# A batch-normalised convolution on one core: a shorter start-up, parameters in PSUM, and one weight sum moved to VectorE by way of PSUM

## The chip, the cores and the metric

The kernel runs on one core of a Trainium2 chip. The metric is the device time of one execution in microseconds (us). The kernel before was timed three times: 195.16, 195.81 and 196.03 us, a median of 195.81 us. The core has five engines that each take their instructions strictly in the order in which the kernel issues them: TensorE (PE in the profile; its weight loads are listed as PEld), VectorE (DVE), ScalarE (ACT), GpSimd (POOL) and SyncE (SP), which here only issues DMAs. A semaphore holds an instruction back until the instructions that it depends on are done, and with it everything behind it on its engine.

## The reference

A convolution of width 3 along the sequence, then a batch norm with stored statistics, then SiLU. All inputs are bf16.

```
B, S, C = 2, 2048, 1024
K = 3
xp = jnp.pad(x, ((0, 0), (P, P), (0, 0)))                      # P = K // 2 = 1
y = sum(jnp.einsum('bsc,cd->bsd', xp[:, k:k + S, :], w[k]) for k in range(K))
inv_std = 1.0 / jnp.sqrt(var + 1e-5)
y = (y - mean) * (g * inv_std) + b
return _silu(y)
```

## The kernel before

The convolution is computed in a transformed domain. Six outputs along the sequence are one tile; a batch of 2048 rows has NTB = 342 tiles. Each tile's 8 input rows are turned into 8 values (points j = 0 to 7) by the 8 x 8 matrix BT, the three weight taps are turned into 8 weight matrices, the products over the 1024 input channels are taken point by point, and 8 products give back 6 outputs. That is 8 products of [1024 x 1024] for 6 rows in place of 18.

**Set-up.** `Rm` (lines 99 to 136) is BT laid out as a [128, 8, 21] matrix, so that one matmul transforms a window of 127 or 128 rows of x, that is 21 tiles, for 128 channels. POOL writes index differences (`val`, line 101), VectorE turns them into an indicator `E` (line 104) and builds rows 1 to 6 of `Rm` from it in 25 small multiply-adds (line 116); POOL writes rows 0 and 7 (line 128) and the identity `ident`. `xw0`, the first window, needs a zero first row, which POOL clears (line 98).

**First stage: the transform of batch 0** (lines 337 to 353). For each of 17 windows, SP loads 128 rows of x (lines 202, 203, 206), TensorE does 8 matmuls (line 216, one for each block of 128 channels, four of them in two PSUM banks), and ScalarE (line 230) or VectorE (line 232) copies the halves to `T_sb` as bf16. The weights of the first output chunk (128 output channels; three taps, `load_chunk`, line 88) are loaded after windows 1 and 2, and the four parameter vectors by POOL's queue (line 178). `turn_params` (line 180), issued ahead of the last window, transposes the parameters in PSUM on TensorE, and VectorE copies them to SBUF (`prmT`, line 183); `make_params` (line 185) computes scale and bias on POOL.

**Weights.** For each chunk dc, `pair_weights` (line 153) makes six transformed weight matrices `uch` of [128, 8 x 128] in three pairs, on POOL: e1 = w0 + w2, then e1 + w1 and e1 - w1; e2 = w0 + 4 w2, then e2 + 2 w1 and e2 - 2 w1; eh = 4 w0 + w2, then eh + 2 w1 and eh - 2 w1. The multiples (`w2x`, `w1x`, `w0x`) are made by `scale_weights` (line 141) on ScalarE, for chunk 0 on POOL. Points 0 and 7 use w0 and w2 as they are.

**Second stage and the rest.** A `unit` (line 251) is one chunk and one batch: 64 matmuls (line 241) of 342 columns, eight for each point, in the order 1, 3, 2, 4, 5, 7, 6, 0, into columns 0 to 341 of four PSUM banks (A, B_, C_, G); units take the lower and the upper four banks in turn. ScalarE copies some products out (line 280) and VectorE combines them with multiply-adds (line 273) into six output rows `y`; the last two of these in a unit write `y[0]`. ScalarE applies scale, bias and SiLU (line 317), partly after the next unit has begun (`late`), the DMA queue transposes, and SP stores. The first unit, (0, 0), is interleaved with the transform of batch 1 (lines 361 to 371), 52 of its matmuls spread over the 17 windows. Then come the units (0, 1), (1, 0), (1, 1) to (7, 1), all bound in order on TensorE (lines 415 to 432). Ahead of each unit (dc, 1), `open_chunk`, `pair_weights` and `scale_weights` issue the weight work of chunk dc + 1 (lines 418 to 427); it stands in each engine's queue behind the work of unit (dc, 0) and ahead of that of unit (dc, 1). The order of all instructions is the order of the program's text (`manual_schedule`, line 60); the framework adds the semaphore waits. `ps_all` (line 69) is a single tile over all 8 banks of PSUM.

Of the kernel before, what the change touches and what calls it, by code (L numbers as in the profile page):

```python
# [9 lines left out]
ALU = mybir.AluOpType  # L10
FP32 = mybir.dt.float32
BF16 = mybir.dt.bfloat16
# [4 lines left out]
BT = [  # L17
# [8 lines left out]
]  # L26
C1 = -2.0 / 9.0
# [3 lines left out]
NJ = 8  # L31
WT = 21
# [3 lines left out]
def kernel(  # L36
# [50 lines left out]
    def load_chunk(dc, k):  # L87
        nc.sync.dma_start(out=raw[dc][k], in_=w_all[:, k, :, dc * P:(dc + 1) * P])  # L88

    open_weights(0)  # L90

    dummy = consts.tile([P, 2], FP32, name="dummy")
    nc.vector.memset(dummy, 0.0)
    nc.scalar.activation(dummy[:, 1:2], dummy[:, 0:1], ACT.Silu)


    xw0 = consts.tile([P, C], BF16, name="xw0")
    nc.gpsimd.memset(xw0[0:1, :], 0.0)
    Rm = consts.tile([P, NJ, WT], BF16, name="Rm")
    val = consts.tile([P, NJ, WT], I32, name="val")  # L100
    nc.gpsimd.iota(val, pattern=[[-1, NJ], [-M_OUT, WT]], base=0, channel_multiplier=1)
    E = consts.tile([P, NJ, WT], FP32, name="E")
    nc.vector.memset(Rm, 0.0)
    nc.vector.tensor_single_scalar(E, val, 0.0, op=ALU.is_equal)
    for k in range(NJ):
        j = 1
        while j < 7:
            v = BT[j][k]
            if v == 0:
                j += 1  # L110
                continue
            j1 = j
            while j1 + 1 < 7 and BT[j1 + 1][k] == v:
                j1 += 1
            nj = j1 - j + 1
            nc.vector.scalar_tensor_tensor(  # L116
                out=Rm[:, j:j1 + 1, :],
                in0=E[:, k:k + 1, :].to_broadcast([P, nj, WT]) if nj > 1 else E[:, k:k + 1, :],
                scalar=float(v),
                in1=Rm[:, j:j1 + 1, :],  # L120
                op0=ALU.mult,
                op1=ALU.add,
            )
            j = j1 + 1
# [12 lines left out]
    ident = consts.tile([P, P], BF16, name="ident")  # L137
    make_identity(nc, ident)
    yTs = [consts.tile([P, M_OUT, NP], BF16, name=f"yT{i}") for i in range(2)]

    def scale_weights(dc, taps=(2, 1, 0), on_gpsimd=False):
        for k in taps:
            f = 2.0 if k == 1 else 4.0
            dst = wx[dc, k] = wtmp.tile([P, CT, P], BF16, name=f"w{k}x")
            if on_gpsimd:
                nc.gpsimd.tensor_scalar(dst, raw[dc][k], f, 0.0, op0=ALU.mult, op1=ALU.add)
            else:
                nc.scalar.mul(dst, raw[dc][k], f)  # L148

    def open_chunk(dc):  # L150
        wts[dc] = upool.tile([P, 6, CT, P], BF16, name="uch")

    def pair_weights(dc, n):

        w0, w1, w2 = raw[dc]
        e = wtmp.tile([P, CT, P], FP32, name=("e1", "e2", "eh")[n])
        a = wx[dc, 0] if n == 2 else w0
        c = wx[dc, 2] if n == 1 else w2
        odd = wx[dc, 1] if n else w1
        nc.gpsimd.tensor_tensor(e, a, c, op=ALU.add)  # L160
# [4 lines left out]
    load = {"act": 0.0, "dve": 1.0}  # L165
    EVAC = {"act": (0.17, 0.14), "dve": (0.12, 0.17)}

    prm = consts.tile([4 * DC, P], BF16, name="prm")
    prmT = consts.tile([P, 4, DC], FP32, name="prmT")
# [6 lines left out]
    def load_params():  # L176
        for q, ap in enumerate((var, g, mean, b)):
            nc.gpsimd.dma_start(out=prm[q * DC:(q + 1) * DC, :], in_=ap.rearrange("(dc p) -> dc p", p=P))

    def turn_params(bk):  # L180
        pv = ps_all[:, bk * 512:bk * 512 + 2 * DC].bitcast(BF16)
        nc.tensor.transpose(pv, prm, ident[0:4 * DC, 0:4 * DC])
        nc.vector.tensor_copy(prmT.rearrange("p q d -> p (q d)"), pv)

    def make_params():
        nc.gpsimd.memset(mhalf, -0.5)
        nc.gpsimd.tensor_scalar(rstd, prmT[:, 0, :], 1e-5, 1.0, op0=ALU.add, op1=ALU.mult)
        nc.gpsimd.tensor_tensor(rstd, rstd, mhalf, op=ALU.pow)
        nc.gpsimd.tensor_tensor(sc, prmT[:, 1, :], rstd, op=ALU.mult)
        nc.gpsimd.tensor_tensor(beta, prmT[:, 2, :], sc, op=ALU.mult)  # L190
        nc.gpsimd.tensor_tensor(beta, prmT[:, 3, :], beta, op=ALU.subtract)
        nc.gpsimd.tensor_scalar(sk, sc, C1, 0.0, op0=ALU.mult, op1=ALU.add)

    epool = ctx.enter_context(tc.tile_pool(name="epool", bufs=1))

    def load_window(xpool, bi, wi):
        ntile = min(WT, NTB - WT * wi)
# [138 lines left out]
    with tc.tile_pool(name="xwin", bufs=10) as xpool:  # L336
        for wi in range(NWIN):
            window = load_window(xpool, 0, wi)
            if wi == 1:
                load_chunk(0, 0)  # L340
                load_chunk(0, 2)
                load_params()
            if wi == 2:
                load_chunk(0, 1)
            for h in range(2):
                transform(0, wi, window, 4 * h, 4, (2 * wi + h) % 4 * 2, 2)
            if wi == 5:
                open_chunk(0)
                for n, taps in ((0, ()), (1, (2, 1)), (2, (0,))):
                    scale_weights(0, taps, on_gpsimd=True)  # L350
                    pair_weights(0, n)
            if wi == NWIN - 2:
                turn_params((2 * wi + 2) % 4 * 2)
        make_params()
        for yT in yTs:
            nc.gpsimd.memset(yT[:, :, NTB:NP], 0.0)

        first = unit(0, 0, 0, NTB, (0, 1, 2, 3), yTs[0], late, seven_first=True)
        load["act"] = load["dve"] = 0.0
        gi, done = 0, 0  # L360
        for wi in range(NWIN):
            window = load_window(xpool, 1, wi)
            if wi == 6:
                for k in (0, 2, 1):
                    load_chunk(1, k)
            for ct0, n in ((0, 3), (3, 3), (6, 2)):
                transform(1, wi, window, ct0, n, 4 + gi % 4, 3)
                gi += 1
                want = 52 * gi // (3 * NWIN)
                run(first, want - done)  # L370
                done = want
        load_weights(1)
        run(first)
# [146 lines left out]
```

## Time and profile before

| What | Value |
|---|---|
| timed runs | 195.16, 195.81, 196.03 us |
| the profiled execution's own time | 196.92 us |
| its span, first to last instruction | 195.1 us |
| granted TensorE clock, mean | 0.979 |
| TensorE busy | 177.8 us (91%) |
| POOL busy | 164.7 us (84%) |
| VectorE busy | 149.4 us (77%) |
| ScalarE busy | 124.2 us (64%) |
| HBM read and written | 14.82 and 8.39 MB |

The span is 1.8 us shorter than the execution's own time, and that execution was 1.1 us longer than the median of the timed runs. A busy share is a mean over stages with different limits: TensorE waits in the first 23 us and in the last 10, and hardly between. In the views that follow, a row gives the start and the length in us, the engine, the line of the code, the operation with its output and inputs, how many instructions are merged in it, and in brackets the idle time ahead of it with what ended it.

### The profile page before, as it was taken

What the parts mean: (1) busy time and instruction counts of PE and PEld (TensorE: products, weight loads), DVE (VectorE), ACT (ScalarE), POOL (GpSimd) and SP (SyncE); (2) the same over time, 40 slices, a digit from 0 to 9 for tenths busy, and PEclk for the clock granted to TensorE, in tenths of its full rate; (3) what the DMA queues carried; (4) which work ended last, traced back from release to release, by engine and by line L of the source; (5) the groups of instructions that cost most, each with busy time, mean ns of one, the idle gap of its engine ahead of it and who ended that gap; (6) DMA issues with size and microseconds to landing.
All of it is one profiled execution on the core that took longest, in us unless ns stands there. A gap on an engine that the chain in (4) does not pass through costs nothing.

```text
span 195.1 us, 3898 instructions
## 1 busy us (share of the span) xinstructions
PE 177.8 (91%) x1397; PEld 126.7 (65%) x1397; DVE 149.4 (77%) x345; ACT 124.2 (64%) x206; POOL 164.7 (84%) x105
## 2 busy tenths in 40 slices
PE   0779799989999999999999999999999999999840
PEld 0668588856666666666666666666666666679830
DVE  6369668996878696969696969686877878697880
ACT  3479558878378827873786287548736872827930
POOL 7899999999999999999999999999999999800000
PEclk9999879999999999999999999999999999999995
DMA  4999999900607487999292989774755657397505
GB/s 135 277 392 344 332 257 371 284 15 2 116 5 137 96 159 182 276 166 200 39 211 41 198 229 257 142 157 92 139 112 116 129 105 152 76 174 157 115 5 108
DMA packets 86823, 31.72 MB, mean 163 GB/s; under 512 B 73428, under 2 KB 82644, under 8 KB 86804
## 3 DMA queue, kind: packets, MB, share of 16 engines
q1 hardware_dynamic: 86637, 31.46, 69.8%
q8 instruction: 11, 0.18, 0.3%
q14 instruction: 8, 0.07, 0.1%
q0 software_dynamic: 128, 0.01, 0.0%
q10 hardware_dynamic: 39, 0.01, 0.0%
HBM read 14.82 MB, written 8.39 MB: 119 GB/s over the span
## 4 chain that ended last, share of the span: by engine, by line
PE 84%; DVE 7%; DMA 3%; SPq 2%; ACT 1%; issue 1%; DVEq 0%; ACTq 0%
PE ps_all L241 76%; PE ps_all L216 7%; DVE T_sb L232 4%; DMA xw<-in_x_dram 3%; DVE y L273 1%; SPq L206 1%; SPq L88 1%; PE ps_all L446 1%; DVE o_end L478 1%; DVE o_end L486 0%; ACT m L280 0%; ACT yT L317 0%; SPq L203 0%; SPq L202 0%; DVE ps_all L273 0%
## 5 line engine op out<-in xcount | busy, mean ns | idle before, releaser
L241 PE MATMUL ps_all<-T_sb,uch 128*128 128x342 bf16 (+2 forms) x816 | 123.9, 299 | 1.8 <-ACT m L280 1.8
L241 PEld LDWEIGHTS <-uch 128*128 128x128 bf16 x816 | 76.7, 97 | 34.5 <-issue 1.3
L317 ACT ACTIVATE yT<-y,beta,sk 128x684 bf16<-128x684 f32 (+8 forms) x51 | 47.1, 925 | 29.9 <-DVE y L273 29.8
L273 DVE SCALAR_TENSOR_TENSOR y<-ps_all,y 128x342 f32<-128x342 f32 (+2 forms) x102 | 45.4, 487 | 1.3
L241 PE MATMUL ps_all<-T_sb,wch 128*128 128x342 bf16 (+2 forms) x272 | 44.7, 303 | 0.1
L216 PE MATMUL ps_all<-Rm,xw 128*128 128x168 bf16 (+1 forms) x272 | 31.8, 248 | 8.5 <-DVE Rm L116 5.4
L280 ACT COPY m<-ps_all 128x342 f32<-128x342 f32 (+2 forms) x51 | 21.7, 427 | 20.6 <-PE ps_all L241 19.6
L230 ACT CAST T_sb<-ps_all 128x672 bf16<-128x672 f32 (+5 forms) x45 | 26.2, 606 | 13.0 <-PE ps_all L216 12.0
L216 PEld LDWEIGHTS <-xw 128*128 128x128 bf16 (+1 forms) x272 | 24.1, 104 | 14.9 <-POOL ident masks.py:199 5.4
L241 PEld LDWEIGHTS <-wch 128*128 128x128 bf16 x272 | 26.0, 98 | 11.6 <-DVE T_sb L232 0.3
L232 DVE CAST T_sb<-ps_all 128x672 bf16<-128x672 f32 (+3 forms) x40 | 26.1, 698 | 8.4 <-PE ps_all L216 8.2
L273 DVE SCALAR_TENSOR_TENSOR d<-m,ps_all 128x342 f32<-128x342 f32 (+2 forms) x17 | 8.3, 490 | 21.0 <-ACT s L280 21.0
L273 DVE SCALAR_TENSOR_TENSOR y<-ps_all,d 128x342 f32<-128x342 f32 (+2 forms) x51 | 22.0, 486 | 0.6
L273 DVE SCALAR_TENSOR_TENSOR y<-ps_all,s 128x342 f32<-128x342 f32 (+2 forms) x34 | 15.2, 489 | 6.3 <-ACT s L280 6.3
L161 POOL TENSOR_TENSOR uch<-e,w1x 128x1024 bf16<-128x1024 f32 x8 | 17.0, 2131 | 1.2 <-ACT w1x L148 0.7
L160 POOL TENSOR_TENSOR e<-wch 128x1024 f32<-128x1024 bf16 x8 | 17.0, 2125 | 0.8 <-DMA wch<-in_w_dram 0.8
L161 POOL TENSOR_TENSOR uch<-eh,w1x 128x1024 bf16<-128x1024 f32 x8 | 17.0, 2131 | 0.6
L161 POOL TENSOR_TENSOR uch<-e,wch 128x1024 bf16<-128x1024 f32 x8 | 17.0, 2129 | 0.6
L160 POOL TENSOR_TENSOR e<-wch,w2x 128x1024 f32<-128x1024 bf16 x8 | 17.0, 2125 | 0.3 <-ACT w2x L148 0.2
L160 POOL TENSOR_TENSOR eh<-w0x,wch 128x1024 f32<-128x1024 bf16 x8 | 17.0, 2124 | 0.1
L162 POOL TENSOR_TENSOR uch<-e,wch 128x1024 bf16<-128x1024 f32 x8 | 17.1, 2133 | 0.0
L162 POOL TENSOR_TENSOR uch<-eh,w1x 128x1024 bf16<-128x1024 f32 x8 | 17.1, 2132 | 0.0
(46 smaller groups left out, 113.6 us busy)
## 6 DMA issues: line engine op xcount, KB each, us to landing
xw<-in_x_dram SPq DMA_DIRECT2D x30, 256.0 KB
out_dram<-o_sb SPq DMA_DIRECT2D x28, 192.0 KB
wch<-in_w_dram SPq DMA_DIRECT2D x9, 512.0 KB
out_dram<-o_sb SPq DMA_DIRECT2D x14, 120.0 KB
wch<-in_w_dram SPq DMA_DIRECT2D x6, 256.0 KB
xw<-in_x_dram SPq DMA_DIRECT2D x2, 224.0 KB
out_dram<-o_before SPq DMA_DIRECT2D x2, 192.0 KB
o_sb<-yT SPq DMA_TRANSPOSE x14
```

The source lines that it names most:

```text
L88: nc.sync.dma_start(out=raw[dc][k], in_=w_all[:, k, :, dc * P:(dc + 1) * P])
L160: nc.gpsimd.tensor_tensor(e, a, c, op=ALU.add)
L161: nc.gpsimd.tensor_tensor(wts[dc][:, 2 * n], e, odd, op=ALU.add)
L162: nc.gpsimd.tensor_tensor(wts[dc][:, 2 * n + 1], e, odd, op=ALU.subtract)
L206: nc.sync.dma_start(out=xw[0:kk, :], in_=x[bi, t_lo:t_hi + 1, :])
L216: nc.tensor.matmul(banks[:, at:at + NJ * ntile], lhsT=xw[0:kk, (ct0 + c) * P:(ct0 + c + 1) * P], rhs=Rm[0:kk, :, 0:ntile], start=True, sto ...
L230: nc.scalar.copy(dst, src)
L232: nc.vector.tensor_copy(dst, src)
L241: nc.tensor.matmul(ps_all[:, bk * 512:bk * 512 + c1 - c0], lhsT=lhsT, rhs=T_sb[bi][:, ct, j, c0:c1], start=start and ct == 0, stop=ct == C ...
L273: nc.vector.scalar_tensor_tensor(out=o, in0=i0, scalar=s, in1=i1, op0=ALU.mult, op1=op1)
L280: nc.scalar.copy(dst, src)
L317: nc.scalar.activation(yT[:, i0:i1:2, c0:c1], y_all[:, i0:i1:2], ACT.Silu, bias=beta[:, dc:dc + 1], scale=sk[:, dc:dc + 1],)
```

## The change: what it does

- **A shorter build of `Rm`.** Rows 1 to 6 come in pairs with equal even and opposite odd parts. Each pair now takes four multiply-adds by way of a helper tile `parts`, 12 in all for the 25. Only rows 0 and 7 are cleared first. The zero row of `xw0` is cleared by VectorE after the build, not by POOL ahead of it.
- **Parameters.** Their four loads go to ScalarE's queue at the very start, ahead of its table load. The transpose follows window 0. The transposed parameters stay in PSUM, in columns 496 to 511 of bank 0, and are read there. VectorE adds the epsilon, POOL takes the power, and VectorE computes scale and bias after the last window.
- **Dummy matmuls.** A zeroed tile `warm` and seven matmuls of 512 columns into bank 7, ahead of the first window.
- **First weights.** The three loads of chunk 0 are issued after windows 3, 5 and 7 instead of 1, 1 and 2; their pair work is issued after window 7 instead of 5.
- **The second pair's sum** for chunks 1 to 7: ScalarE writes 4 w2 as fp32 to columns 352 to 479 of all eight PSUM banks, and VectorE adds w0 to it. POOL's addition for this pair is gone, and so is the `w2x` multiple. ScalarE's multiples of w1 and w0 are now issued ahead of all three pairs.
- **Smaller things.** The clearing of the padding in `yTs` moves to the start of POOL's queue, and the first unit's matmuls are spread one transform group later.

```diff
+    prm = consts.tile([4 * DC, P], BF16, name="prm")
+    for q, ap in enumerate((var, g, mean, b)):
+        nc.scalar.dma_start(out=prm[q * DC:(q + 1) * DC, :], in_=ap.rearrange("(dc p) -> dc p", p=P))
+
     dummy = consts.tile([P, 2], FP32, name="dummy")
...
-    xw0 = consts.tile([P, C], BF16, name="xw0")
-    nc.gpsimd.memset(xw0[0:1, :], 0.0)
     Rm = consts.tile([P, NJ, WT], BF16, name="Rm")
     val = consts.tile([P, NJ, WT], I32, name="val")
     nc.gpsimd.iota(val, pattern=[[-1, NJ], [-M_OUT, WT]], base=0, channel_multiplier=1)
+    xw0 = consts.tile([P, C], BF16, name="xw0")
     E = consts.tile([P, NJ, WT], FP32, name="E")
-    nc.vector.memset(Rm, 0.0)
+    parts = consts.tile([P, 3, 2, WT], FP32, name="parts")
+    warm = consts.tile([P, 512], BF16, name="warm")
+    nc.vector.memset(warm, 0.0)
+    nc.vector.memset(Rm[:, 0:NJ:NJ - 1, :], 0.0)
     nc.vector.tensor_single_scalar(E, val, 0.0, op=ALU.is_equal)
-    for k in range(NJ):
...
+    for n, odd in enumerate((1.0, 2.0, 0.5)):
+        row = BT[2 * n + 1]
+        assert [odd * row[k + 1] for k in (1, 3, 5)] == row[1:6:2] and row[6] == 1
+        rstt(parts[:, n], E[:, 1:3], row[2], E[:, 5:7])
+        rstt(parts[:, n], E[:, 3:5], row[4], parts[:, n])
+        rstt(Rm[:, 2 * n + 1], parts[:, n, 0], odd, parts[:, n, 1])
+        rstt(Rm[:, 2 * n + 2], parts[:, n, 0], -odd, parts[:, n, 1])
+    nc.vector.memset(xw0[0:1, :], 0.0)
...
+    for yT in yTs:
+        nc.gpsimd.memset(yT[:, :, NTB:NP], 0.0)
...
-        c = wx[dc, 2] if n == 1 else w2
+        c = wx[dc, 2] if n == 1 and not dc else w2
         odd = wx[dc, 1] if n else w1
-        nc.gpsimd.tensor_tensor(e, a, c, op=ALU.add)
+        if n == 1 and dc:
+            four = ps_all.rearrange("p (k e) -> p k e", e=512)[:, :, 352:352 + P]
+            nc.scalar.mul(four, w2, 4.0)
+            nc.vector.scalar_tensor_tensor(out=e, in0=four, scalar=1.0, in1=w0, op0=ALU.mult, op1=ALU.add)
+        else:
+            nc.gpsimd.tensor_tensor(e, a, c, op=ALU.add)
         nc.gpsimd.tensor_tensor(wts[dc][:, 2 * n], e, odd, op=ALU.add)
         nc.gpsimd.tensor_tensor(wts[dc][:, 2 * n + 1], e, odd, op=ALU.subtract)
...
-    def turn_params(bk):
-        pv = ps_all[:, bk * 512:bk * 512 + 2 * DC].bitcast(BF16)
-        nc.tensor.transpose(pv, prm, ident[0:4 * DC, 0:4 * DC])
-        nc.vector.tensor_copy(prmT.rearrange("p q d -> p (q d)"), pv)
+    prmT = ps_all[:, 512 - 2 * DC:512].bitcast(BF16).rearrange("p (q d) -> p q d", q=4)
+
+    def turn_params():
+        nc.tensor.transpose(prmT.rearrange("p q d -> p (q d)"), prm, ident[0:4 * DC, 0:4 * DC])
+        nc.vector.tensor_scalar(rstd, prmT[:, 0, :], 1e-5, 1.0, op0=ALU.add, op1=ALU.mult)
+        nc.gpsimd.tensor_tensor(rstd, rstd, mhalf, op=ALU.pow)
 
     def make_params():
...
+        nc.vector.tensor_tensor(sc, prmT[:, 1, :], rstd, op=ALU.mult)
+        nc.vector.tensor_tensor(beta, prmT[:, 2, :], sc, op=ALU.mult)
+        nc.vector.tensor_tensor(beta, prmT[:, 3, :], beta, op=ALU.subtract)
+        nc.vector.scalar_tensor_tensor(out=sk, in0=prmT[:, 1, :], scalar=C1, in1=rstd, op0=ALU.mult, op1=ALU.mult)
+
+    nc.gpsimd.memset(mhalf, -0.5)
...
+    for _ in range(7):
+        nc.tensor.matmul(ps_all[:, 7 * 512:8 * 512], lhsT=warm[:, 0:P], rhs=warm, start=True, stop=True)
...
-            if wi == 1:
-                load_chunk(0, 0)
-                load_chunk(0, 2)
-                load_params()
-            if wi == 2:
-                load_chunk(0, 1)
+            if wi in (3, 5, 7):
+                load_chunk(0, {3: 0, 5: 2, 7: 1}[wi])
             for h in range(2):
                 transform(0, wi, window, 4 * h, 4, (2 * wi + h) % 4 * 2, 2)
-            if wi == 5:
+            if wi == 0:
+                turn_params()
+            if wi == 7:
...
-            if wi == NWIN - 2:
-                turn_params((2 * wi + 2) % 4 * 2)
         make_params()
...
-                want = 52 * gi // (3 * NWIN)
+                want = 52 * max(gi - 1, 0) // (3 * NWIN - 1)
...
             open_chunk(dc + 1)
-            pair_weights(dc + 1, 0)
-            if dc == 0:
-                scale_weights(1, (2,), on_gpsimd=True)
-                scale_weights(1, (1, 0))
-            else:
-                scale_weights(dc + 1)
-            for n in (1, 2):
+            scale_weights(dc + 1, (1, 0))
+            for n in range(3):
                 pair_weights(dc + 1, n)
```

More of the change, by code (lines that the diff above doesn't have):

```diff
@@ L101, with rstt @@
     nc.gpsimd.iota(val, pattern=[[-1, NJ], [-M_OUT, WT]], base=0, channel_multiplier=1)
+    xw0 = consts.tile([P, C], BF16, name="xw0")
     E = consts.tile([P, NJ, WT], FP32, name="E")
-    nc.vector.memset(Rm, 0.0)
+    parts = consts.tile([P, 3, 2, WT], FP32, name="parts")
+    warm = consts.tile([P, 512], BF16, name="warm")
+    nc.vector.memset(warm, 0.0)
+    nc.vector.memset(Rm[:, 0:NJ:NJ - 1, :], 0.0)
     nc.vector.tensor_single_scalar(E, val, 0.0, op=ALU.is_equal)
-    for k in range(NJ):
[L106 to L124, printed above, removed]
+    def rstt(o, i0, f, i1):
+        nc.vector.scalar_tensor_tensor(out=o, in0=i0, scalar=float(f), in1=i1, op0=ALU.mult, op1=ALU.add)
+    for n, odd in enumerate((1.0, 2.0, 0.5)):
[6 more added lines that the diff above has]
+    nc.vector.memset(xw0[0:1, :], 0.0)
     for j in (0, 7):
@@ L166 @@
     EVAC = {"act": (0.17, 0.14), "dve": (0.12, 0.17)}
-    prm = consts.tile([4 * DC, P], BF16, name="prm")
-    prmT = consts.tile([P, 4, DC], FP32, name="prmT")
     sk = consts.tile([P, DC], FP32, name="sk")
@@ L174 @@
     sc = consts.tile([P, DC], FP32, name="sc")
-    def load_params():
-        for q, ap in enumerate((var, g, mean, b)):
-            nc.gpsimd.dma_start(out=prm[q * DC:(q + 1) * DC, :], in_=ap.rearrange("(dc p) -> dc p", p=P))
-    def turn_params(bk):
-        pv = ps_all[:, bk * 512:bk * 512 + 2 * DC].bitcast(BF16)
-        nc.tensor.transpose(pv, prm, ident[0:4 * DC, 0:4 * DC])
-        nc.vector.tensor_copy(prmT.rearrange("p q d -> p (q d)"), pv)
-    def make_params():
[L186 to L192, printed above, removed]
+    prmT = ps_all[:, 512 - 2 * DC:512].bitcast(BF16).rearrange("p (q d) -> p q d", q=4)
[3 more added lines that the diff above has]
+        nc.gpsimd.tensor_tensor(rstd, rstd, mhalf, op=ALU.pow)
+    def make_params():
+        nc.vector.tensor_tensor(sc, prmT[:, 1, :], rstd, op=ALU.mult)
[3 more added lines that the diff above has]
+    nc.gpsimd.memset(mhalf, -0.5)
     epool = ctx.enter_context(tc.tile_pool(name="epool", bufs=1))
+    for _ in range(7):
+        nc.tensor.matmul(ps_all[:, 7 * 512:8 * 512], lhsT=warm[:, 0:P], rhs=warm, start=True, stop=True)
     def load_window(xpool, bi, wi):
@@ L351 @@
                     pair_weights(0, n)
-            if wi == NWIN - 2:
-                turn_params((2 * wi + 2) % 4 * 2)
         make_params()
-        for yT in yTs:
-            nc.gpsimd.memset(yT[:, :, NTB:NP], 0.0)
         first = unit(0, 0, 0, NTB, (0, 1, 2, 3), yTs[0], late, seven_first=True)
```

## The prediction

> **What bounds the kernel now.** I read the chain that ended last first (by line, then in order of time), then the first 24 us, then one boundary between units, then the granted clock.
>
> ```profile
> PE 84%; DVE 7%; DMA 3%; SPq 2%; ACT 1%; issue 1%; DVEq 0%; ACTq 0%
> ...
> 42.59 137.20 PE ps_all L241 x958
> ```
>
> From 42.6 to 179.8 us TensorE runs 958 matmuls with no gap, 0.143 us each. So in that stretch every stall of TensorE is paid in full, and nothing taken from another engine is gained. What can be gained lies ahead of 22.7 us, where the first of these matmuls starts:
>
> ```profile
> 5.40 2.40 PE L216 MATMUL ps_all<-Rm,xw 128*128 128x168 bf16 x16 [5.40 <-DVE Rm L116]
> 8.29 1.30 PE L216 MATMUL ps_all<-Rm,xw 128*128 128x168 bf16 x8 [0.50 <-DMA xw<-in_x_dram]
> 10.91 9.74 PE L216 MATMUL ps_all<-Rm,xw 128*128 128x168 bf16 x104 [1.32 <-DMA xw<-in_x_dram]
> ...
> 21.83 0.70 PE L216 MATMUL ps_all<-Rm,xw 33*128 33x48 bf16 x11 [1.06 <-DVE prmT L183]
> 22.66 0.32 PE L241 MATMUL ps_all<-T_sb,wch 128*128 128x342 bf16 x1
> ```
>
> The start waits for `Rm`, then for x behind the early weight loads; from 10.9 us on, 13 windows go at the pace of the copies (0.746 us for a half on ScalarE, 0.852 on VectorE): 10.26 us from the first at 11.42 to the last's end at 21.68, 0.79 a window; then the parameters cost a 1.06 us wait. POOL bounds nothing: no TensorE wait names a weight tile.
>
> **The start, part by part.** (a) `Rm`: 25 multiply-adds took 2.91 us from 2.34 on. The iota is no longer behind POOL's 0.94 us clearing, so `E` starts about 0.9 us sooner; 12 operations at 0.12 to 0.2 us (lengths 0.178 and 0.201) are 1.4 to 2.4 us, and the row of `xw0` adds 0.3 to 0.9 us: ready at 3.6 to 4.6. (b) Seven dummies of 512 columns, at the 0.15 us per 168 columns seen at 5.4 us (2.40 / 16), are 3.2 us from about 1.2 on: the queue frees at 4.4. The first x matmul moves from 5.40 to about 4.4. (c) The transpose behind window 0 waits for ScalarE's first copy of bank 0 and for four loads that now precede a 1.28 us table load; ScalarE is ready near 4.5 and the transpose at about 6; window 1 waits behind it. (d) The bytes up to the last window are the same 5.0 MB; at the 387 GB/s of the windows from 11 to 16 us that is 12.9 us, so x cannot all land before about 16. Weights after windows 3, 5 and 7 let windows 2 and 3 come without the 0.50 and 1.32 us waits. From a copy start near 6.6, 15 windows at 0.79 are 11.9, and the short window 0.4 more: the first product at about 18.9 instead of 22.66, a gain of **3.8** (bounds 1.5, if x still sets the pace late, to 6, if x alone does). This contains the 1.06 us wait; the four small VectorE steps of `make_params` now stand ahead of batch 1's copies, some 0.5 us there.
>
> POOL starts chunk 0 later, when w0 and w2 land (8.5 to 9.5 instead of 7.6) and w1 (10 to 12). From 11.9, point 3's weights come at 22.5 and point 5's at 30.0 by the rows of 2.12 and 1.04; TensorE wants them at about 24.3 and 32. Nothing is paid while w1 lands before about 13.5; a microsecond later costs a microsecond.
>
> A rule of the skill about the dummies: the Trainium skill, "TensorE: Matmul & The Clock Gate" (What's actually happening), says that the array stays at half clock until about 3.4 us of sustained work, so dummies of 3 us would end just short of it. The granted clock reads 1.00 there and cannot show it, though the 0.15 us spacing does. By the page, an estimate: up to 1 us of (b) is lost. By the rows nothing is, since x sets the pace behind it.
>
> The clock also dips once, as the granted-clock column (the 0.99, 0.50 and 1.00 ahead of the DMA share and GB/s) shows:
>
> ```profile
> 19.90:23.30 3.40, 2.19 (x27) 1.56 (x25) 2.24 (x6) 1.96 (x4) 3.31 (x3) 0.99 1.05 361
> 23.30:26.70 3.40, 3.40 (x22) 2.73 (x20) 1.87 (x3) 1.45 (x3) 3.24 (x3) 0.50 1.08 219
> 26.70:30.10 3.40, 3.40 (x39) 2.93 (x38) 2.96 (x5) 2.46 (x6) 3.40 (x2) 1.00 0.96 314
> ```
>
> About 2 us with little matmul work (20.65 to 22.66) are followed by 3.4 us at half clock, 1.7 us lost. With the parameter wait gone this may or may not recur: I take **1.0** gained (0 to 1.7).
>
> **The second pair's sum: the part that decides.** POOL loses 2.12 us in each of seven chunks, worth nothing, as POOL is waited for nowhere. But the path to that sum runs through PSUM. ScalarE's 4 w2 lies in columns 352 to 479 of every bank, and units use columns 0 to 341 of the same banks. In the instruction lists of the built kernels, which name the semaphore count each instruction waits for, three waits are new at each of the seven boundaries from unit (dc, 0) to (dc, 1): ScalarE's write waits for VectorE's last `y[0]` of unit (dc, 0); VectorE's sum waits for that write; and the first matmul of unit (dc, 1) waits for that sum. Their columns don't meet; the banks do. Queued behind that matmul is all of TensorE's work. The rows of one boundary:
>
> ```profile
> 60.26 1.06 ACT L148 ACTIVATE w2x<-wch 128x1024 bf16<-128x1024 bf16 x1
> ...
> 63.14 3.65 PE L241 MATMUL ps_all<-T_sb,uch 128*128 128x342 bf16 x24
> ...
> 65.77 0.52 DVE L273 SCALAR_TENSOR_TENSOR y<-ps_all,y 128x342 f32<-128x342 f32 x1
> ```
>
> Today unit (1, 1) starts at 63.14, while VectorE ends `y[0]` at 66.29, 3.15 later. In the changed kernel the write starts at 66.3: 1.06 by the `w2x` row, the same elements written to SBUF (bounds 0.9 to 1.4: the 672-element copy out of PSUM, 0.746, would give 1.1 by its length). The sum is 1024 elements in fp32; the 342-column multiply-adds take 0.508 and those of 245 columns 0.41, 1.0 ns an element, so 1.2 (bounds 1.1 to 1.5). With two hand-overs of 0.03 to 0.05, the stall is 3.15 + 1.06 + 1.2 + 0.1 = **5.5 us**. Unit (0, 0) ends its products at 44.56 and `y[0]` at 47.33, so there 2.77 + 2.36 = 5.1. Seven: 6 x 5.45 + 5.1 = **37.8** (bounds 4.6 and 6.2 each: 32 to 43). No cover hides it: the next matmul in order is the one that waits. ScalarE's late SiLU of the unit stands behind the write too, but unit (dc, 1) has not begun, so nothing waits for it. POOL's pair 2 starts with the sum, and has 11 us until unit (dc + 1, 0).
>
> A rule that speaks against this change: the Trainium skill, "PSUM — Partial Sum Buffer" (PSUM bank collisions raise a hardware error), says that PSUM must be guarded by bank, not by address, as two engines in one bank at once collide even on disjoint columns. By it these waits are needed and the sum holds; were columns enough, the stalls would be 0. The only row here of TensorE held by a small PSUM reader is the 1.06 us above.
>
> Each stall is longer than the 2 us that cost the clock at 23.3, so I charge the same 3.4 us at half clock behind each: 1.7 lost, seven times **11.9** (0 if it stays up, 3.4 each if two such windows pass).
>
> **Sum**, against the profiled execution's 196.92 us: - 3.8 - 1.0 + 37.8 + 11.9 = + 44.9, so 241.8; that execution was 1.1 above the median of the runs shown, so **241.0** on their footing.
>
> **The rivals.**
> 1. Stalls without the clock's part: 241.0 - 11.9 = 229.1. For it: the dip at 23 us is a single case. Against: its gap was less than half as long as these.
> 2. Two half-clock windows at each stall: 241.0 + 11.9 = 252.9. For it: a 5.5 us gap may spoil two windows. Against: the busy window after the one dip restored the clock at once.
> 3. Faster: the boundary costs nothing, because the new waits end before TensorE gets there. It is decided at VectorE's `y[0]`: the write, the sum and so TensorE would have to be done by 63.14, that is `y[0]` by 60.8 instead of 66.3. Then the time is 195.8 - 4.8 = 191.0. For it: ScalarE's multiples do run at 60.3, within its 3.17 us of idle time in other units. Against: `y[0]` needs point 0, TensorE's last product in the unit, so only a wait read wrongly by me makes it so.
>
> **How the numbers follow.** Main case 76%, rival 1 10%, rival 2 7%, rival 3 7%. The bounds of the main case are -7 and +8 from the stalls and the start, and the clock fills the way towards rivals 1 and 2: 230 to 250 leaves out rival 3, rival 2 and part of rival 1, about 2 in 10. 0.5% (1 us) is what a measurement of this kernel can tell from no change. Faster 6%, same 1%, slower 93%: rival 3 alone is not slower.
>
> **What would show it.** Right: TensorE's list of waits has the unit's line waiting seven times for VectorE's weight sum, some 5.5 us each, 38 in all; half clock follows each; the chain of waits goes through the last `y[0]`, the PSUM write and the sum; TensorE's first product is near 19; POOL's busy time falls by some 15 us of the 164.7. Wrong: if the dense stretch is still one unbroken piece of 137 us, the waits don't bind, and if TensorE waits there for POOL, the covers that I granted to POOL were not there.

## The result, and the profile after

| | before | after |
|---|---|---|
| median of the runs, us | 195.92 (4 runs, 195.16 to 197.64) | 249.64 (4 runs, 249.21 to 250.14) |
| profiled execution, us | 196.92 | 249.42 |
| its span, us | 195.1 | 247.6 |
| its mean granted clock of TensorE | 0.979 | 0.910 |

The time is 1.2712 times that of before (95% interval 1.2658 to 1.2765): slower, as forecast, and 8.6 us above the forecast of 241.0. The page of the changed kernel, first its span in 40 slices, then the shares of the chain that ended last, then the new group on ScalarE:

```profile
PE   7688898299919995699649982999299955999960
...
PEclk9999999779995999799958997699959997999997
...
PE 62%; DVE 17%; DMA 7%; ACT 6%; issue 4%; SPq 3%; DVEq 0%; ACTq 0%
...
L163 ACT ACTIVATE ps_all<-wch 128x1024 f32<-128x1024 bf16 x7 | 7.2, 1027 | 26.9 <-DVE y L277 24.3
```

TensorE's unbroken stretch from 42.6 to 179.8 us is gone: its row now has seven dips, and the clock row dips beside each. VectorE's share of the last chain rises from 7% to 17% and ScalarE's from 1% to 6%. Ahead of the seven writes into PSUM ScalarE sat idle for 26.9 us; for six of them, 24.3 us in all, the trace names `y` of VectorE as what ended the wait, for one (2.6 us) it names nothing. TensorE's list of waits (us in total, times, longest) names the other end:

```profile
PE ps_all L245 <- DVE e L164: 37.5, 7, 5.4
PE ps_all L220 <- DMA xw<-in_x_dram: 3.5, 4, 1.0
PE ps_all L245 <- ACT m L284: 1.8, 3, 0.8
```

The first row is new: `L245` is the unit's matmul, `L164` the weight sum. One boundary in the timeline shows how the 5.4 us come about (start, length, then engine and line; in brackets the idle time ahead and what ended it):

```profile
98.56 0.52 DVE L277 SCALAR_TENSOR_TENSOR y<-ps_all,y 128x342 f32<-128x342 f32 x1
99.10 1.03 ACT L163 ACTIVATE ps_all<-wch 128x1024 f32<-128x1024 bf16 x1 [4.05 <-DVE y L277]
...
100.23 1.23 DVE L164 SCALAR_TENSOR_TENSOR e<-ps_all,wch 128x1024 f32<-128x1024 f32 x1 [1.16 <-ACT ps_all L163]
101.51 1.87 PE L245 MATMUL ps_all<-T_sb,uch 128*128 128x342 bf16 x6 [5.42 <-DVE e L164]
```

Each row starts 0.02 to 0.1 us after the one above ends: last `y[0]`, PSUM write, weight sum, first matmul of the next unit. TensorE had stopped at 96.09 (101.51 - 5.42), 2.99 us before `y[0]` ended at 99.08; so it waits out the tail of the old unit and then the whole detour of the weights.

TensorE comes back at half clock. Stretches of the same trace, around the boundary above and around the next one (from:to, length, busy time and count of TensorE, its weight loads, VectorE, ScalarE and POOL, then granted clock, DMA share and GB/s):

```profile
100.80:101.50 0.70, 0.00 (x0) 0.00 (x0) 0.66 (x1) 0.21 (x1) 0.00 (x0) 0.50 0.00 1
101.50:104.10 2.60, 2.59 (x10) 1.38 (x10) 0.00 (x0) 0.11 (x1) 2.56 (x2) 0.50 0.00 0
104.20:107.60 3.40, 3.40 (x25) 2.23 (x23) 0.26 (x1) 2.44 (x5) 3.40 (x2) 1.00 0.00 0
...
124.70:126.90 2.20, 0.00 (x0) 0.00 (x0) 1.23 (x1) 1.76 (x2) 0.00 (x0) 0.50 0.01 1
126.95:131.50 4.55, 4.55 (x17) 2.40 (x17) 0.00 (x0) 0.44 (x1) 4.52 (x3) 0.50 0.00 0
131.60:135.00 3.40, 3.40 (x26) 2.23 (x24) 0.91 (x2) 2.82 (x5) 3.32 (x2) 1.00 0.00 0
```

At 101.51 the clock is low for 2.7 us after the restart, at 126.95 for 4.6. Over the seven restarts (47.92, 74.54, 101.51, 126.95, 153.33, 180.15, 207.22) it is low for 5.1, 5.8, 2.7, 4.6, 5.5, 6.0 and 2.8 us: 32.4 us in all, of which half, **16.2 us**, is lost work.

The start moved less than forecast:

```profile
4.16 1.26 PE L220 MATMUL ps_all<-Rm,xw 128*128 128x168 bf16 x8
5.87 0.17 PE L184 MATMUL ps_all<-ident,prm 32*128 32x32 bf16 x1 [0.45 <-ACT T_sb L234]
5.97 2.15 PE L220 MATMUL ps_all<-Rm,xw 128*128 128x168 bf16 x24
8.90 1.55 PE L220 MATMUL ps_all<-Rm,xw 128*128 128x168 bf16 x16 [0.77 <-DVE T_sb L236]
11.46 1.52 PE L220 MATMUL ps_all<-Rm,xw 128*128 128x168 bf16 x16 [1.00 <-DMA xw<-in_x_dram]
14.02 6.62 PE L220 MATMUL ps_all<-Rm,xw 128*128 128x168 bf16 x72 [1.04 <-DMA xw<-in_x_dram]
21.31 0.60 PE L220 MATMUL ps_all<-Rm,xw 128*128 128x168 bf16 x6 [0.67 <-DMA xw<-in_x_dram]
21.74 0.31 PE L245 MATMUL ps_all<-T_sb,wch 128*128 128x342 bf16 x1
...
41.52 1.32 PE L245 MATMUL ps_all<-T_sb,wch 128*128 128x342 bf16 x8
```

The first window of x starts at 4.16 in place of 5.40, but at 8.90, 11.46 and 14.02 pairs of windows follow each other at 2.56 us: two windows and one load of weights between them. By 20.6 us little of the lead is left: here batch 0's short last window ends at 20.64, before, the window ahead of it ended at 20.65. The first product is at 21.74 in place of 22.66. The last weight group of the first unit starts at 41.52, 1.9 us earlier than in the kernel before:

```profile
43.40 1.32 PE L241 MATMUL ps_all<-T_sb,wch 128*128 128x342 bf16 x8
```

Together: - 1.9 + 37.5 + 16.2 = + 51.8 of the + 52.5 us between the two spans; 0.7 us is not assigned.

### The profile page after: what moved, and what is told of

The parts are those of the page before. It is cut to its first block, busy times and chain, and to the rows that moved or that the text cites. A ratio compares the mean times of both kernels' runs of the same rounds, so it can differ in the third digit from the quotient of the medians.

```text
span 247.6 us, 3888 instructions
## 1 busy us (share of the span) xinstructions
PE 195.3 (79%) x1404; PEld 130.8 (53%) x1404; DVE 158.3 (64%) x345; ACT 125.8 (51%) x207; POOL 144.6 (58%) x87
## 4 chain that ended last, share of the span: by engine, by line
PE 62%; DVE 17%; DMA 7%; ACT 6%; issue 4%; SPq 3%; DVEq 0%; ACTq 0%
PE ps_all L245 58%; DVE y L277 10%; DMA xw<-in_x_dram 7%; DVE e L164 3%; PE ps_all L220 3%; ACT ps_all L163 3%; SPq L210 2%; DVE ps_all L277 2%; DVE y L309 1%; ACT yT L321 1%; ACT s L284 1%; ACT m L284 1%; SPq L88 1%; DVE o_end L470 0%; ACT w0x L149 0%
## 5 line engine op out<-in xcount | busy, mean ns | idle before, releaser
L245 PE MATMUL ps_all<-T_sb,uch 128*128 128x342 bf16 (+2 forms) x816 | 139.5, 325 | 39.3 <-DVE e L164 37.5
L245 PEld LDWEIGHTS <-uch 128*128 128x128 bf16 x816 | 82.6, 104 | 83.0 <-issue 40.3
L167 POOL TENSOR_TENSOR uch<-e,w1x 128x1024 bf16<-128x1024 f32 x8 | 17.0, 2122 | 65.2 <-DVE e L164 65.1
L245 PE MATMUL ps_all<-T_sb,wch 128*128 128x342 bf16 (+2 forms) x272 | 43.8, 300 | 0.0
L220 PE MATMUL ps_all<-Rm,xw 128*128 128x168 bf16 (+1 forms) x272 | 29.7, 236 | 4.6 <-DMA xw<-in_x_dram 3.5
L245 PEld LDWEIGHTS <-wch 128*128 128x128 bf16 x272 | 25.7, 97 | 11.3
L220 PEld LDWEIGHTS <-xw 128*128 128x128 bf16 (+1 forms) x272 | 21.8, 99 | 11.9 <-DMA xw<-in_x_dram 5.9
L163 ACT ACTIVATE ps_all<-wch 128x1024 f32<-128x1024 bf16 x7 | 7.2, 1027 | 26.9 <-DVE y L277 24.3
```

Of the source, the lines that this page charges most:

```text
L163: nc.scalar.mul(four, w2, 4.0)
L220: nc.tensor.matmul(banks[:, at:at + NJ * ntile], lhsT=xw[0:kk, (ct0 + c) * P:(ct0 + c + 1) * P], rhs=Rm[0:kk, :, 0:ntile], start=True, sto ...
L245: nc.tensor.matmul(ps_all[:, bk * 512:bk * 512 + c1 - c0], lhsT=lhsT, rhs=T_sb[bi][:, ct, j, c0:c1], start=start and ct == 0, stop=ct == C ...
```

## The experiments

Theory: the second pair's sum costs all of the loss, because its PSUM columns lie in banks that TensorE and VectorE still use, so a chain of three waits crosses each boundary; and the idle time then costs the clock. The rest of the change is a small gain. In what follows "the kernel before" was run on the same chip beside each experiment (medians 196.18 to 196.50), and a ratio is to that. Every diff is against the changed kernel unless it says otherwise.

### The sum taken out, and the sum alone

`e1_sum_back`: the second pair's sum is back on POOL with `w2x`, and the order of pairs and multiples as before; the rest of the change stays.

```diff
-        c = wx[dc, 2] if n == 1 and not dc else w2
+        c = wx[dc, 2] if n == 1 else w2
...
-        if n == 1 and dc:
-            four = ps_all.rearrange("p (k e) -> p k e", e=512)[:, :, 352:352 + P]
-            nc.scalar.mul(four, w2, 4.0)
-            nc.vector.scalar_tensor_tensor(out=e, in0=four, scalar=1.0, in1=w0, op0=ALU.mult, op1=ALU.add)
-        else:
-            nc.gpsimd.tensor_tensor(e, a, c, op=ALU.add)
+        nc.gpsimd.tensor_tensor(e, a, c, op=ALU.add)
```

> The changed kernel with the second pair's sum back on POOL (with its w2x multiple, as before); the start stays changed. Theory (the PSUM boundary costs everything): no wait of TensorE at the unit boundaries, no half clock behind them, and what is left is the start: first product at 21.7 and end of the first unit at 42.7 instead of 44.6, so 194.0 us (193.3 to 194.8). Rival (the start lost something too that the stalls hide, for instance POOL late with chunk 7, whose slack before was 2.0 us): 196 or more, with TensorE waiting for POOL.

Measured: 195.37 us (12 runs), 0.9952 of before (0.9922 to 0.9981).

`e2_sum_alone`: the kernel before with the PSUM sum and its order of issue, and nothing else of the change.

> The kernel before with only the second pair's sum changed (ScalarE's write to all eight banks, VectorE's sum). Theory: seven stalls of 5.1 to 5.4 us (37.5 in all) and half clock behind each (15.8 lost in the profiled run of the changed kernel): 195.9 + 53.3 = 249.2 us (245 to 253). Rival (the stalls need the new start as well): under 230.

Measured: 250.99 us (2 runs), 1.2775 (1.2685 to 1.2865). TensorE's waits in it:

```profile
PE ps_all L246 <- DVE e L163: 37.5, 7, 5.4
```

The same seven waits with the same sum as in the full change. So the sum alone makes the loss, and all the other parts together are worth 1.1 us (196.50 to 195.37): small, but the interval stops short of 1. The forecast for them was 4.8. That `e1_sum_back` came out 1.4 us slower than expected says the same: the start was over-estimated.

### PSUM, or VectorE's extra work?

`e3_four_sbuf` keeps ScalarE's multiple and VectorE's sum, and the early order of issue, and only puts 4 w2 into SBUF, as bf16.

```diff
-            four = ps_all.rearrange("p (k e) -> p k e", e=512)[:, :, 352:352 + P]
+            four = wtmp.tile([P, CT, P], BF16, name="w2x")
```

> The changed kernel, but ScalarE's 4 w2 goes to an SBUF tile in bf16 and VectorE adds w0 from there: same engines, same order, no PSUM. Theory (banks): stalls gone, 194.0 us (193.3 to 194.8). Rival (VectorE's 1.24 us at the end of its queue is the cost, wherever it reads): seven times 1.2 us or more, 202 us upwards, 3.15 + 1.2 per boundary if the matmuls still had to wait for it: about 225 us.

Measured: 195.32 us (12 runs), 0.9941 (0.991 to 0.9972), with no wait of a unit's matmul for a weight sum. Its longest lists of waits:

```profile
ACT yT L321 <- DVE y L277: 29.4, 16, 3.2
ACT m L284 <- PE ps_all L245: 19.4, 29, 0.9
POOL uch L167 <- DVE e L164: 15.8, 7, 5.9
```

POOL still waits for VectorE's sum, 15.8 us in place of 65.1, but that is hidden. VectorE is as busy as in the changed kernel (157.3 and 158.3 us). So the place of 4 w2 makes the 54 us, not VectorE's work and not the order. (The type changes with the place, fp32 to bf16; that alone was not tried.)

`e7_direct` drops the intermediate tile: VectorE multiplies and adds from the raw weights in one instruction.

```diff
-            four = ps_all.rearrange("p (k e) -> p k e", e=512)[:, :, 352:352 + P]
-            nc.scalar.mul(four, w2, 4.0)
-            nc.vector.scalar_tensor_tensor(out=e, in0=four, scalar=1.0, in1=w0, op0=ALU.mult, op1=ALU.add)
+            nc.vector.scalar_tensor_tensor(out=e, in0=w2, scalar=4.0, in1=w0, op0=ALU.mult, op1=ALU.add)
```

> The changed kernel with the second pair's sum on VectorE straight from the raw weights in SBUF (w2 times 4, plus w0, in one instruction): no PSUM and no write by ScalarE. Theory (only the PSUM banks bound): as e3, 195.3 us on the footing of a kernel before at 196.5 (0.994 of it, 0.990 to 0.997), ScalarE 7 us less busy, worth nothing. Rival (ScalarE's queue matters at the boundaries): faster than e3 by 1 us or more.

Measured: 195.32 us (12 runs), 0.9946 (0.9912 to 0.998), the same as `e3_four_sbuf`. One ScalarE instruction a chunk saved is worth nothing here: it was hidden.

### Which banks: a miss

A unit uses four of the eight banks, 0 to 3 and 4 to 7 in turn. `e4_early_half` puts 4 w2 only into banks 0 to 3, those of the unit that is ending, in two passes of 512 elements; `e5_late_half` is the same with banks 4 to 7 (`4 * 512:8 * 512`), those of the unit that is to start.

```diff
-            four = ps_all.rearrange("p (k e) -> p k e", e=512)[:, :, 352:352 + P]
-            nc.scalar.mul(four, w2, 4.0)
-            nc.vector.scalar_tensor_tensor(out=e, in0=four, scalar=1.0, in1=w0, op0=ALU.mult, op1=ALU.add)
+            four = ps_all[:, 0 * 512:4 * 512].rearrange("p (k e) -> p k e", e=512)[:, :, 352:352 + P]
+            for h in (0, 4):
+                nc.scalar.mul(four, w2[:, h:h + 4], 4.0)
+                nc.vector.scalar_tensor_tensor(out=e[:, h:h + 4], in0=four, scalar=1.0, in1=w0[:, h:h + 4], op0=ALU.mult, op1=ALU.add)
```

> The changed kernel, the sum still through fp32 PSUM at columns 352 to 479, but in two passes through banks 0 to 3 only (the banks of the unit that has just ended) and not through banks 4 to 7, which the next unit uses. Theory (what counts is which banks are shared): the first matmul of the next unit waits for nothing new; VectorE is held some 2.5 us, half of it idle time; 194 to 195 us. Rival (PSUM traffic beside the matmuls, or VectorE's time, is the cost): 220 us or more.

Measured: 235.14 us (6 runs), 1.1974 (1.1913 to 1.2034), 40 us above what was expected. The first row is TensorE's largest wait, the others are from the timeline of one boundary:

```profile
PE ps_all L246 <- ACT m L285: 29.2, 10, 4.0
```

```profile
66.17 2.49 PE L246 MATMUL ps_all<-T_sb,uch 128*128 128x342 bf16 x16
...
68.80 0.52 DVE L278 SCALAR_TENSOR_TENSOR y<-ps_all,y 128x342 f32<-128x342 f32 x1
...
69.34 0.60 ACT L164 ACTIVATE ps_all<-wch 128x512 f32<-128x512 bf16 x1 [4.05 <-DVE y L278]
...
70.76 0.60 ACT L164 ACTIVATE ps_all<-wch 128x512 f32<-128x512 bf16 x1 [0.81 <-DVE e L165]
71.30 0.94 ACT L322 ACTIVATE yT<-y,beta,sk 128x684 bf16<-128x684 f32 x1
...
72.14 0.77 ACT L285 COPY m<-ps_all 128x342 f32<-128x342 f32 x2
...
72.62 4.72 PE L246 MATMUL ps_all<-T_sb,uch 128*128 128x342 bf16 x16 [3.96 <-ACT m L285]
```

What was expected of TensorE happened: it crosses the boundary without a stop and does two groups of eight matmuls of the new unit from 66.17 on. What was left out is ScalarE's own queue. Its PSUM write still waits for the last `y[0]` (4.05 us), and behind it in order stands the `m` copy of the new unit's first group, which TensorE's next matmul needs. The wait that no longer held TensorE directly held it one step later, through an engine that executes in order: 3.96 us in place of 5.42. The seven boundaries make 27.4 of the 29.2 us (the other 1.8, in three places, were there before), and by the trace's clock records half clock takes some 12 us more: together the 40.

> Like e4 (fp32 PSUM, two passes, columns 352 to 479), but in banks 4 to 7, those of the unit that starts next; banks 0 to 3 are free for TensorE. The first write no longer waits for the last y[0], the first matmul waits for the second pass of VectorE's sum: 3.15 + 0.69 + 0.6 + 0.69 + hand-overs = 5.3 us a boundary (4.9 to 5.6), half clock behind each (2.2): 195.3 + 7 x 7.5 = 248 us (243 to 252). Theory of the held matmul and theory of the held ScalarE queue (e4) agree on the time; they differ in who is named: here VectorE's sum.

Measured: 244.26 us (2 runs), 1.2427 (1.2314 to 1.2539); span 242.1, and the wait is on the unit's first matmul again:

```profile
PE ps_all L246 <- DVE e L165: 34.5, 7, 5.0
```

ScalarE's first write no longer waits for `y[0]` here; VectorE's first sum stands behind `y[0]` in its own queue, the second write waits for that sum, and TensorE for the second sum. So in this pair the matmul waits where the sum reads the banks that the matmul will write, 4 to 7, and not where it reads 0 to 3, though in both the columns (352 to 479 against 0 to 341) never meet.

### What the lost clock is worth

`e6_late_dummies` is `e5_late_half` with matmuls of zeroes ahead of the held one, into a bank of the old half, so that TensorE is busy while it would wait:

```diff
+        if bi == 1 and dc + 1 < DC:
+            for _ in range(32):
+                nc.tensor.matmul(ps_all[:, 512:512 + NTB], lhsT=warm[:, 0:P], rhs=warm[:, 0:NTB], start=True, stop=True)
```

> e5 with 32 dummy matmuls of 342 columns (4.6 us) into bank 1 ahead of the held matmul, so that TensorE works through most of the wait. Theory (the half clock behind each stall comes from TensorE's idleness and costs 1.4 to 2.9 us each, 15.8 in all): granted clock 1.0 throughout, the waits themselves as in e5, so 195.3 + 37 = 232 us (229 to 236), 16 less than e5. Rival (the slow stretch behind a stall is the wait's own doing, or the dummies add their time): equal to e5 or above.

Measured: 232.39 us (2 runs), 1.1823 (1.1715 to 1.193), 11.9 us below `e5_late_half`, where 16 was expected. Its clock row and its wait:

```profile
PEclk9999999999999999999999999999999999999995
```

```profile
PE ps_all L246 <- DVE e L165: 2.1, 6, 0.3
```

No half clock is left in the middle, and 2.1 us of wait; the rest of the 34.5 is filled with matmuls that compute nothing. The span of 229.5 is still 36.0 above the 193.5 of `e3_four_sbuf`. So both parts are real and add up: the held queue costs its own length, and the idleness of TensorE costs the clock on top of it, about 12 us there.

### The start: what the other parts are worth

All of these start from `e3_four_sbuf`, so that the boundaries are quiet. `e8_early_weights` loads chunk 0 as in the kernel before, two loads after window 1 and one after window 2:

```diff
-            if wi in (3, 5, 7):
-                load_chunk(0, {3: 0, 5: 2, 7: 1}[wi])
+            if wi == 1:
+                load_chunk(0, 0)
+                load_chunk(0, 2)
+            if wi == 2:
+                load_chunk(0, 1)
```

> e3 with the first weights' loads back at windows 1, 1 and 2. Theory (the loads cost the x stream the same transfer time wherever they stand, and the copies set the rest): first product within 0.5 us of e3's 22.7, time equal to e3's within 0.5%. Rival (the later loads are what gained): 1 us or more slower than e3, about the kernel before. Other rival (early loads fill the time in which Rm is built): faster by 1 us.

Measured: 195.20 us (10 runs), 0.9943 (0.9913 to 0.9972).

`e9_no_dummies` leaves out the seven dummy matmuls.

> e3 without the seven dummy matmuls. Theory (x sets the pace, so the clock of the first windows is worth nothing): equal to e3 within 0.5%, first matmuls 0.15 us apart until about 9 us. Rival (the dummies save up to 1 us): 1 us slower.

Measured: 195.29 us (12 runs), 0.9949 (0.992 to 0.9978).

`e10_weights_5_7_9` and `e11_weights_7_9_11` issue the three loads later still, with the pair work after the last of them:

```diff
-            if wi in (3, 5, 7):
-                load_chunk(0, {3: 0, 5: 2, 7: 1}[wi])
+            if wi in (5, 7, 9):
+                load_chunk(0, {5: 0, 7: 2, 9: 1}[wi])
```

> e3 with the first weights after windows 5, 7 and 9. Theory (copies of windows behind a load starve, so later loads starve fewer): first product 0.5 to 1.5 us sooner, 0 to 1 us faster than e3. Rival (POOL's first chunk, some 1.5 us later, is waited for at point 3): TensorE waits for POOL, equal or slower.

> e3 with the first weights after windows 7, 9 and 11. Theory: first product 1 to 2.5 us sooner, but point 3's weights come at about 25.5 against a need near 25: equal to e3 or up to 1.5 us faster. Rival (POOL late): TensorE waits 1 us or more for POOL in the first unit, slower than e10.

Measured: 195.28 us (10 runs), 0.9933 (0.9903 to 0.9962), and 196.42 us (12 runs), 0.998 (0.995 to 1.0009). After windows 5, 7, 9 nothing is gained, where up to 1 us was thought possible; after 7, 9, 11 what the change gains is lost again, with a 0.7 us wait for POOL's `uch` in the trace. Both first products came later than that of `e3_four_sbuf` (23.54 and 23.26 against 22.68), where 0.5 to 2.5 us sooner was expected.

None of the four gets below 195.2, so neither the later weights nor the dummies are what makes the 1.1 us; which other part does was not separated. Their first products lie at 22.64, 21.34, 23.54 and 23.26 us, and the last weight group of the first unit at 41.75, 41.94, 42.78 and 43.21: `e9_no_dummies` leads `e8_early_weights` by 1.3 us at the first product and is 0.2 behind twenty microseconds later. These are single traces. The changed kernel, `e7_direct`, `e3_four_sbuf` and `e1_sum_back` have the same start, and their first products lie at 21.74, 22.20, 22.68 and 22.83, their last groups at 41.52, 42.78, 41.93 and 41.63; so a microsecond between two traces proves little, and the order at the first product is not kept there either. In the timeline of `e9_no_dummies`, which has the earliest first product, TensorE's rows say where it goes:

```profile
21.34 0.32 PE L243 MATMUL ps_all<-T_sb,wch 128*128 128x342 bf16 x1
...
29.14 0.39 PE L218 MATMUL ps_all<-Rm,xw 128*128 128x168 bf16 x3 [1.10 <-DMA xw<-in_x_dram]
...
32.86 0.39 PE L218 MATMUL ps_all<-Rm,xw 128*128 128x168 bf16 x3 [0.36 <-DMA xw<-in_x_dram]
...
40.23 0.31 PE L243 MATMUL ps_all<-T_sb,uch 128*128 128x342 bf16 x1 [0.71 <-POOL uch L168]
```

TensorE waits twice for the second batch's x (the 0.71 at 40.23 stands in the other traces too, there for ScalarE's `m`). In the queue that loads it the three loads of chunk 1 were issued from 20.46 to 24.81, ahead of ten windows of x. `e12_second_weights` is `e9_no_dummies` with just these three moved:

```diff
-            if wi == 6:
+            if wi == 12:
                 for k in (0, 2, 1):
                     load_chunk(1, k)
```

> The kernel without the dummies (4 w2 in SBUF, weights of chunk 0 after windows 3, 5 and 7), with the three loads of chunk 1 issued after window 12 of the second batch in place of window 6. If the loads of weights between the windows of x are what gives the earlier start back, the waits for x at 29 and 33 us (1.10 and 0.36 there) go, the last weight group of the first unit starts near 40.5 in place of 41.94, and the time falls to 0.987 to 0.99 of the kernel before (193.6 to 194.3). Rival, the pace of x as a whole: the waits stay or move later, the last group stays at 41.6 to 42, and the time stays at 0.994 to 0.996. If POOL has chunk 1 too late, a wait for POOL shows at the unit's line behind 60 us.

Measured: 193.77 us (11 runs), 0.9892 (0.9856 to 0.9927). The profiled execution was the longest of the eleven, 195.22 us. Its trace has half clock from 14.8 to 18.2 us, which that of `e9_no_dummies` doesn't have; whether that made it the longest stays open, as another execution of 195.19 us had a mean clock of 0.993. Its rows:

```profile
23.02 0.32 PE L243 MATMUL ps_all<-T_sb,wch 128*128 128x342 bf16 x1 [0.21 <-DVE T_sb L234]
...
40.10 0.31 PE L243 MATMUL ps_all<-T_sb,uch 128*128 128x342 bf16 x1 [0.71 <-ACT m L282]
...
41.81 1.32 PE L243 MATMUL ps_all<-T_sb,wch 128*128 128x342 bf16 x8
```

It starts its products 1.68 us later than `e9_no_dummies` and reaches the last weight group 0.13 us earlier: 18.8 us between the two against 20.6, without the waits for x. No wait for POOL appears behind 60 us. But the last group was expected near 40.5, and 41.81 is what the rival expected; and products that start 1.68 us later would have been spared most of the 1.10 and 0.36 us of waiting in any case. What the loads do to x is seen in the DMA packets of the two traces: window 7 of batch 1, the first behind the three loads in `e9_no_dummies`, has landed 3.8 us after window 6 there (28.3 after 24.5) and 0.8 us after it in `e12_second_weights` (25.0 after 24.2). So the loads do hold x up by about 3 us, and the time fell as the theory expected. That this is where the 1.5 us between the medians come from is likely but not shown: the one profiled execution does not have them, and the ratios' intervals of `e9_no_dummies` and `e12_second_weights` still touch (0.992 and 0.9927). `e12_second_weights` is the fastest version found, 1.1% below the kernel before.

## Why the prediction was right, and where it was off

- **The three waits across the boundary.** Right in place and size: 37.8 forecast, 37.5 measured. ScalarE's write took 1.03 (1.06 forecast by the `w2x` row), VectorE's sum 1.23 (1.2), the tail of `y[0]` 2.99 (3.15), the first boundary 5.07 (5.1). The doubt kept open, that the waits might be read wrongly (rival 3), is settled by `e2_sum_alone` and `e3_four_sbuf`.
- **Bank or column.** The Trainium skill, "PSUM — Partial Sum Buffer" (PSUM bank collisions raise a hardware error), asks that PSUM be guarded by bank, since a different address in the same bank collides as well. The waits of this program follow banks: with 4 w2 in banks 4 to 7 the matmul waits 34.5 us in seven places, with banks 0 to 3 it does not wait for the sum. What the hardware would do without the waits was not tried.
- **The half clock: mechanism right, size off.** The step "3.4 us at half clock behind each: 1.7 lost, seven times 11.9" should have been 16.2. It took the length of the one dip in the trace of before for the length of all. In the trace, the low clock lasts 3.4 us in two cases and 6.8 us in five, the two windows of rival 2, and only the part after the restart costs time.
- **What decides between one and two windows.** At the two short cases (101.51 and 207.22) the clock had fallen 0.72 and 0.62 us before TensorE came back; at the five long ones 0.85 to 2.3 us before. The clock records of `e2_sum_alone`, `e4_early_half` and `e5_late_half` have 21 more such pauses, of 3.6 to 5.4 us, and they sort the same way. Of the 28, the 14 in which TensorE came back before the fall or up to 0.76 us after it have 3.41 us of low clock, the 14 in which it came back 0.84 us after it or later have 6.83. The Trainium skill, "TensorE: Matmul & The Clock Gate" (What's actually happening), says that the clock is decided by a free-running window of about 3.4 us, low after an idle one and full after a busy one. The 28 cases agree, if a window counts as busy when TensorE comes back early enough in it; the border lies between 0.76 and 0.84 us of its 3.41. "Idle" does not fit every fall: in the 3.4 us ahead of the dip in the trace of before TensorE was busy for 2.19 (the row 19.90:23.30 above).
- **The start: the largest error against its size.** "The first product at about 18.9 instead of 22.66" came at 21.74; of 3.8 + 1.0 us, 1.9 show in the trace and 1.1 in the time (`e1_sum_back`). The step that failed is "at the 387 GB/s of the windows from 11 to 16 us that is 12.9 us": weights were priced as if they came at the rate of x. Two windows and a load of weights, 256 KB each (786 kB), took 2.56 us, 307 GB/s; with the windows at 387 GB/s (0.68 us each) the load of weights is left with 1.2 us. By the DMA packets the last window of batch 0 had landed at 18.1 us, where the forecast had "about 16", and at 17.7 in the kernel before. Windows 2 and 3 did come without the 0.50 and 1.32 us waits, but nothing was gained by it: the waits moved behind the new places of the loads, 1.00 and 1.04 us at 11.46 and 14.02, and 0.77 at 8.90, where VectorE's copy and x came at the same moment.
- **The gain behind the start.** The forecast let whatever is gained at the first product reach the end. It does not: `e9_no_dummies` waits 1.46 us for the second batch's x on the way, and its lead over `e8_early_weights` is gone at the last group.
- **Covers granted to POOL.** They held, though narrowly: POOL waited 0.44 us for w1 and took its second step at 13.43 us ("about 13.5" was the limit), and no wait of TensorE names a POOL tile in the changed kernel. POOL's busy time fell by 20.1 us (164.7 to 144.6) in place of 15: beside the seven sums (14.8) the clearing of `xw0` (0.94), a `w2x` multiple (1.04), the issue of the parameters' four loads (2.3) and five of their small steps (1.0) left it.
- **The dip at 23 us.** Gone, as taken: the granted clock is 1.00 from 21 to 27.8 us. Elsewhere in these runs a half clock shows between 10 and 20 us instead (`e1_sum_back`, `e3_four_sbuf` and `e12_second_weights` among them), so this gain is not a firm one.
- **The sum.** Against the profiled execution, 241.8 was forecast and 249.42 measured, 7.6 more: 4.3 from the clock, 2.9 from the start, - 0.3 from the stalls, and the 0.7 that is not assigned. To the median: before, the profiled execution was 1.1 us above it; after, 0.2 below. That is 1.3 us more, 8.9 in all, against 240.7; for 241.8 less 1.1 is 240.7, and the prediction's 241.0 is 0.3 too high. (Its sum for `Rm` is off as well: the terms of (a) give 3.1 to 4.7, not 3.6 to 4.6; the tile was complete at 4.08.) The two larger errors, clock and start, point the same way and carried the result to 0.4 us below the upper end of the prediction's 230 to 250. That it still lies inside is partly luck; that the path and the size of the waits came true is not.

## What to carry to other kernels

In a program whose waits go by bank, as here, a free corner of a PSUM bank is not free storage: whoever writes it waits for the bank's last reader, and whoever needs the bank next waits for the writer. So before using it look at which unit owns the bank at that moment, and at what stands behind the write in its own engine's queue. A stall of TensorE is to be priced with its clock: here 5.4 us of waiting cost another 1.4 to 3.0 us each. When a start is shortened, follow the gain to the next stage before counting it; here a lead of 1.3 us at the first product (`e9_no_dummies` over `e8_early_weights`) was gone twenty microseconds later, behind loads of weights queued ahead of x.

## What the runs showed that was not expected

- The half clock at a pause of 3.6 to 5.4 us lasts 3.41 or 6.83 us: in 28 pauses of four traces 3.41 where TensorE resumed no later than 0.76 us after the fall of the clock, 6.83 where it resumed 0.84 us after it or later; in the changed kernel the price of seven nearly equal pauses ran from 1.35 to 3.0 us.
- Matmuls of zeroes keep the clock at full speed through a pause (`e6_late_dummies`: 11.9 us of 244.26); at the start of the kernel the seven dummies bring nothing that can be measured (195.32 with them, 195.29 without).
- A 256 KB load of weights held the stream of x up for about 1.2 us, an estimate from the spacing above (1.0 by the packets of `e9_no_dummies` and `e12_second_weights`), against 0.68 for a window of x of the same size. Moving three such loads behind six more windows lowered the median by 1.5 us, with intervals that just touch.
- Freeing TensorE of a wait while ScalarE still stands in one gained 14.5 us of the 54 (249.64 to 235.14), not all of it: the in-order queue passed the wait on.
